# Four buffers instead of two for the output tiles of a fused attention and feed-forward kernel

## The chip, the cores and the metric

The kernel runs on one core of one Trainium2 chip. A core has five engines with instruction streams of their own: PE (TensorE, matrix products; PEld is its loading of weights, which overlaps the products), DVE (VectorE), ACT (ScalarE), POOL (GpSimd) and SP (SyncE, which here issues every DMA, in order). The metric is the device time of one execution in microseconds; where a kernel was run several times the median counts. All matrix products are in float32, most of them split into a high and a low part of type fp32r, so that one product becomes three.

## What is computed

```python
def sm_attn(qq, kk, vv):
    s = scale * np.matmul(qq, kk.transpose(0, 1, 3, 2))
    s = s - np.max(s, axis=-1, keepdims=True)
    a = np.exp(s)
    a = a / (np.sum(a, axis=-1, keepdims=True) + 1e-09)
    return np.matmul(a, vv)
p_packed = sm_attn(p, k, v)            # 32 packed rows per head
out = sm_attn(q, p_packed, p_packed)   # 8 batches, 8 heads, 576 rows, 64 wide
...
h = x @ w_in                           # x: 4608 x 512, w_in: 512 x 2048
g = np.maximum(h, 0.0) + alpha * np.minimum(h, 0.0)
return (g @ w_out).astype(np.float32)  # w_out: 2048 x 512
```

The attention's output, its heads side by side, is the `x` of the feed-forward part.

## The kernel before

The kernel never forms `x`. For each batch, `packed_w` multiplies the packed rows with `w_in` (the result is `pw`, matmuls on lines L435 to L437, copies on L443), and the feed-forward part multiplies that by the second attention's weights (`a_h`, `a_l`).

The feed-forward part works in **sweeps**. A sweep k covers half a batch, 288 tokens, and there are 16. Within one it runs over f = 0 to 15, sixteen blocks of 128 of d_ff. For each f, `first(k, f)` makes a product in a PSUM tile `ps_h` (L480 to L482, six matmuls of 128x288; L468 in the first two sweeps), and takes it through a chain of four steps: ACT forms `neg` (L486), DVE puts the leaky part together in place (L487), ACT rounds it to `gh` (L492), DVE takes the remainder `gl` (L493). There are two `ps_h` buffers and three each of `gh` and `gl`. `second(k, f)` then multiplies `gh` and `gl` by the block f of `w_out` into four accumulators `acc0` to `acc3`, one for each 128 columns of the output (L505, L506 with `gh`, L507 with `gl`, so twelve matmuls for each f). The accumulators are four PSUM banks, each with one buffer, so the next sweep's first product into one of them waits until it has been copied out.

At f = 15 each accumulator is copied into a tile `ot` from the pool `op`: accumulators 0 and 2 by DVE (L524), 1 and 3 by ACT (L522). In the first two sweeps DVE adds a partial sum instead (L518). SP then sends `ot` to memory (L526, 144 KB each). The pool `op` has two buffers; a third copy waits until the first tile's DMA has landed.

For the other matters named below: L456 and L458 split `pw` into `pwh` and `pwl` (on DVE from batch 2 on), once for every two f. L172 and L173 split the attention's inputs (ACT, POOL), L390 to L392 transpose and split the attention's weights (DVE, ACT, POOL). `w` is a block of `w_in`, loaded by L410 into three buffers.

The loops at the end set the program's order of ideas: `first` runs two steps ahead of `second`, and the attention of later batches is spread between them by a table of starting steps. The order on each engine, however, is not that one. A scheduler, with a model of time of its own, deals the instructions to the engines when the program is built; it knows how many buffers a pool has. So a change of a buffer count moves instructions.

Of the kernel before, what the change touches and what calls it, by code (L numbers as in the profile page):

```python
# [28 lines left out]
def pack_attention_ffn_kernel(  # L29
# [42 lines left out]
    pwj = ctx.enter_context(tc.tile_pool(name="pwj", bufs=2))  # L72
    win = ctx.enter_context(tc.tile_pool(name="win", bufs=3))
    gp = ctx.enter_context(tc.tile_pool(name="gp", bufs=2))
    op = ctx.enter_context(tc.tile_pool(name="op", bufs=2))
    dram = ctx.enter_context(tc.tile_pool(name="dram", bufs=1, space=bass.MemoryType.DRAM))
    ps_a = ctx.enter_context(tc.tile_pool(name="ps_a", bufs=1, space=bass.MemoryType.PSUM))
    ps_h = ctx.enter_context(tc.tile_pool(name="ps_h", bufs=2, space=bass.MemoryType.PSUM))
# [555 lines left out]
```

## Time and profile before

| | |
|---|---|
| runs | 836.61, 836.7, 833.1 us; median 836.61 |
| profiled execution | 834.6 us, of which the span from first to last instruction is 832.8 |
| PE busy | 786.3 us, 94% of the span |
| PEld busy | 731.3 us, 88% |
| DVE busy | 610.6 us, 73% |
| ACT busy | 486.6 us, 58% |
| POOL busy | 208.7 us, 25% |
| mean granted TensorE clock | 0.983 of full speed |

Busy time of PE is modelled, and matmuls overlap each other: one of 128x288 is shown with some 300 ns, but the next starts about 130 ns after it. So a delay of PE is best read from the starts of consecutive matmuls, or from the idle time of PEld. A wait is put down to the instruction that released it last. Most waits of DVE and ACT cost nothing, because PE has work in the meantime.

Three stretches follow each other: a prologue of some 170 us in which weights are converted, a middle up to about 628 us in which the feed-forward sweeps share the engines with the attention of later batches, and a late stretch of pure sweeps. Sweeps end in the middle at 243, 293, 341, 387, 433, 485, 534 and 584 us, later at 631, 674, 713, 751, 790, and the last at 827 us.

### The profile page before, as it was taken

To read this page: it belongs to the slowest core of one execution; us is meant where nothing else is said; L and a number is where in the kernel's file an instruction comes from. 1 tells how busy PE (TensorE), PEld (TensorE's weight loads), DVE (VectorE), ACT (ScalarE), POOL (GpSimd) and SP (SyncE) were. 2 spreads that over 40 slices of the span, in tenths; PEclk is the share of its full clock that TensorE was granted. 3 is DMA by queue.
4 is the path that set the end of the run, shared out by engine and by line. 5 is a ranking of instruction groups with operands and counts; after the bars stand their busy time and mean duration, and the time that the engine had idled before them with its cause. 6 is when DMAs were issued, how large, how long until landed. Compare 5 with 4: busy or idle time off the path is not lost.

```text
span 832.8 us, 14967 instructions
## 1 busy us (share of the span) xinstructions
PE 786.3 (94%) x5384; PEld 731.3 (88%) x5384; DVE 610.6 (73%) x1303; ACT 486.6 (58%) x1141; POOL 208.7 (25%) x203
## 2 busy tenths in 40 slices
PE   5489998999999999999999999899999999999997
PEld 3257686898799989998999999899999999999997
DVE  4999798976777657889786487987955566666663
ACT  5778766756666765665667765555655533333332
POOL 2100022536667302353361024533210000000000
PEclk9779999999999999999999999999999999999999
DMA  9877755555623661321227522300262000000000
GB/s 301 280 234 242 240 187 197 195 180 173 209 89 108 207 211 37 91 72 58 61 86 235 199 86 57 89 27 15 80 204 80 26 30 2 29 1 30 2 29 29
DMA packets 55386, 97.97 MB, mean 118 GB/s; under 512 B 5136, under 2 KB 32784, under 8 KB 55312
## 3 DMA queue, kind: packets, MB, share of 16 engines
q1 hardware_dynamic: 55312, 97.02, 36.0%
q8 instruction: 42, 0.69, 0.3%
q14 instruction: 32, 0.26, 0.1%
HBM read 79.18 MB, written 17.83 MB: 116 GB/s over the span
## 4 chain that ended last, share of the span: by engine, by line
PE 71%; DVE 14%; DMA 6%; ACT 5%; issue 2%; SPq 1%; POOL 0%; ACTq 0%; DVEq 0%
PE acc L505 14%; PE acc L506 13%; PE acc L507 13%; PE ps_h L480 6%; PE ps_h L482 6%; PE ps_h L481 6%; PE ps_h L468 2%; PE ps_m L435 2%; PE ps_m L437 2%; PE ps_m L436 2%; DVE ps_h L487 2%; DMA wraw<-in_w_in 1%; PE ps_m L316 1%; DVE pwl L458 1%; DVE mag L127 1%
## 5 line engine op out<-in xcount | busy, mean ns | idle before, releaser
L505 PE MATMUL acc<-gh,wo 128*128 128x288 f32 x1024 | 289.6, 302 | 11.0 <-ACT gh L492 7.9
L506 PE MATMUL acc<-gh,wo 128*128 128x288 f32 x1024 | 283.4, 295 | 0.0
L505 PEld LDWEIGHTS acc<-gh,wo 128*128 128x128 f32 x1024 | 193.0, 189 | 24.1 <-ACT gh L492 15.8
L507 PE MATMUL acc<-gl,wo 128*128 128x288 f32 x1024 | 205.9, 301 | 0.0
L506 PEld LDWEIGHTS acc<-gh,wo 128*128 128x128 f32 x1024 | 193.3, 189 | 1.5
L492 ACT CAST gh<-ps_h 128x288 fp32r<-128x288 f32 x256 | 102.5, 401 | 123.8 <-DVE ps_h L487 113.2
L486 ACT ACTIVATE neg<-ps_h 128x288 f32<-128x288 f32 x256 | 105.6, 413 | 109.0 <-PE ps_h L482 103.0
L493 DVE TENSOR_TENSOR gl<-ps_h,gh 128x288 fp32r<-128x288 f32 x256 | 115.4, 452 | 72.1 <-ACT gh L492 70.4
L487 DVE SCALAR_TENSOR_TENSOR ps_h<-neg,nal,ps_h 128x288 f32<-128x288 f32 x256 | 132.0, 516 | 44.9 <-ACT neg L486 43.3
L507 PEld LDWEIGHTS acc<-gl,wo 128*128 128x128 f32 x1024 | 159.3, 188 | 3.5
L480 PE MATMUL ps_h<-a_h,pwh 128*128 128x288 f32 x448 | 133.5, 298 | 0.3 <-DVE gl L493 0.2
L482 PE MATMUL ps_h<-a_h,pwl 128*128 128x288 f32 x448 | 131.9, 295 | 0.7 <-POOL pwl L458 0.7
L481 PE MATMUL ps_h<-a_l,pwh 128*128 128x288 f32 x448 | 132.0, 295 | 0.0
L173 POOL TENSOR_TENSOR xl<-xraw,xh 128x576 fp32r<-128x576 f32 x48 | 71.0, 1478 | 136.0 <-ACT xh L172 132.8
L480 PEld LDWEIGHTS ps_h<-a_h,pwh 128*128 128x128 f32 x448 | 84.1, 188 | 2.0 <-DVE gl L493 1.0
L482 PEld LDWEIGHTS ps_h<-a_h,pwl 128*128 128x128 f32 x448 | 83.9, 188 | 1.4 <-POOL pwl L458 1.1
L481 PEld LDWEIGHTS ps_h<-a_l,pwh 128*128 128x128 f32 x448 | 84.1, 188 | 0.5
L458 DVE TENSOR_TENSOR pwl<-pw,pwh 128x512 fp32r<-128x512 f32 x96 | 74.5, 776 | 7.1 <-PE ps_h L482 1.2
L456 DVE CAST pwh<-pw 128x512 fp32r<-128x512 f32 x112 | 54.9, 493 | 29.9 <-PE ps_h L481 27.7
L443 ACT COPY pw<-ps_m 64x512 f32<-64x512 f32 x112 | 65.1, 581 | 17.2 <-PE ps_m L437 13.0
L275 POOL TENSOR_TENSOR vs<-vraw,vs 128x640 fp32r<-128x640 f32 x24 | 38.6, 1610 | 42.3 <-ACT vs L274 41.7
L435 PE MATMUL ps_m<-w,pt 128*128 128x512 f32 (+1 forms) x80 | 33.8, 422 | 12.9 <-ACT w L133 10.6
(112 smaller groups left out, 1029.9 us busy)
## 6 DMA issues: line engine op xcount, KB each, us to landing
w<-w_split SPq DMA_DIRECT2D x64, 512.0 KB, 4.2
xraw<-in_kT SPq DMA_DIRECT2D x32, 288.0 KB, 2.9
xraw<-in_qT SPq DMA_DIRECT2D x32, 288.0 KB, 2.8
outT<-ot SPq DMA_DIRECT2D x64, 144.0 KB, 1.8
vraw<-in_v SPq DMA_DIRECT2D x32, 256.0 KB, 2.9
wraw<-in_w_out SPq DMA_DIRECT2D x16, 512.0 KB, 4.1
wraw<-in_w_in SPq DMA_DIRECT2D x16, 512.0 KB, 4.9
w_split<-w SPq DMA_DIRECT2D x16, 512.0 KB, 4.6
```

The source lines that it names most:

```text
L173: nc.gpsimd.tensor_tensor(out=xl, in0=raw, in1=fv(xh), op=ALU.subtract)
L458: eng.tensor_tensor(out=tl, in0=src, in1=fv(th), op=ALU.subtract)
L480: nc.tensor.matmul(ps[:, :HS], th[:, i, fs], a_h[:, i, tok], start=hi, stop=False)
L481: nc.tensor.matmul(ps[:, :HS], th[:, i, fs], a_l[:, i, tok], start=False, stop=False)
L482: nc.tensor.matmul(ps[:, :HS], tl[:, i, fs], a_h[:, i, tok], start=False, stop=lo)
L486: nc.scalar.activation(out=neg, in_=g, func=AF.Relu, scale=-1.0)
L487: nc.vector.scalar_tensor_tensor(out=g, in0=neg, scalar=nal[:, f : f + 1], in1=g, op0=ALU.mult, op1=ALU.add)
L492: nc.scalar.copy(out=gh, in_=g)
L493: nc.vector.tensor_tensor(out=gl, in0=g, in1=fv(gh), op=ALU.subtract)
L505: nc.tensor.matmul(acc[o][:, :HS], wo_t[f][:, 0, os_], gh, start=begin, stop=False)
L506: nc.tensor.matmul(acc[o][:, :HS], wo_t[f][:, 1, os_], gh, start=False, stop=False)
L507: nc.tensor.matmul(acc[o][:, :HS], wo_t[f][:, 0, os_], gl, start=False, stop=end)
```

## The change

The pool `op` gets four buffers in place of two.

```diff
-    op = ctx.enter_context(tc.tile_pool(name="op", bufs=2))
+    op = ctx.enter_context(tc.tile_pool(name="op", bufs=4))
```

No instruction is added or removed; the scheduler's order changes from the second sweep's end onward. In the rows below, a leading + is the order now, - the order before. `acc_9798` to `acc_9801` are accumulators 0 to 3 of the sweep before the last, `acc_10262` to `acc_10265` those of the last; `wo_330` and `wo_390` are the blocks f = 0 and f = 1 of `w_out`.

On PE, where the last sweep begins (at 790 us before; the late sweep ends are alike):

```order
 L506 MATMUL acc_10263<-gh,wo_330 128x288
 L507 MATMUL acc_10263<-gl,wo_330 128x288
+L505 MATMUL acc_10265<-gh,wo_330 128x288
+L506 MATMUL acc_10265<-gh,wo_330 128x288
+L507 MATMUL acc_10265<-gl,wo_330 128x288
+L505 MATMUL acc_10264<-gh,wo_330 128x288
+L506 MATMUL acc_10264<-gh,wo_330 128x288
+L507 MATMUL acc_10264<-gl,wo_330 128x288
 L505 MATMUL acc_10262<-gh,wo_390 128x288
 L506 MATMUL acc_10262<-gh,wo_390 128x288
 L505 MATMUL acc_10263<-gh,wo_390 128x288
 L506 MATMUL acc_10263<-gh,wo_390 128x288
```

The six f = 0 matmuls of accumulators 2 and 3 now stand ahead of the first f = 1 matmul; before, they came after f = 1 and part of f = 2 of accumulators 0 and 1.

On DVE at the same place:

```order
 L524 COPY ot<-acc_9798 128x288
+L524 COPY ot<-acc_9800 128x288
 L458 TENSOR_TENSOR pwl<-pw,pwh 128x512
 L487 SCALAR_TENSOR_TENSOR ps_h<-neg,nal,ps_h 128x288 x2
-L493 TENSOR_TENSOR gl<-ps_h,gh 128x288
-L524 COPY ot<-acc_9800 128x288
-L493 TENSOR_TENSOR gl<-ps_h,gh 128x288
+L493 TENSOR_TENSOR gl<-ps_h,gh 128x288 x2
 L456 CAST pwh<-pw 128x512
 L458 TENSOR_TENSOR pwl<-pw,pwh 128x512
```

The copy of accumulator 2 has moved from behind L458, two L487 and an L493 to right behind the copy of accumulator 0. On ACT the copy of accumulator 3 has moved in the same way, ahead of one L486 and two L492.

On DVE at the sweep end at 534 us, where attention runs beside the sweep (`acc_6477` and `acc_6479` are accumulators 0 and 2; `s_6464` is the transpose that feeds L391 and L392):

```order
-L456 CAST pwh<-pw 128x512
 L390 STREAM_TRANSPOSE s_6464<-t_6575 128x576
+L493 TENSOR_TENSOR gl<-ps_h,gh 128x288
+L456 CAST pwh<-pw 128x512
 L524 COPY ot<-acc_6477 128x288
 L211 TENSOR_TENSOR s_6592<-ps_m,lo 64x288
+L524 COPY ot<-acc_6479 128x288
 L458 TENSOR_TENSOR pwl<-pw,pwh 128x512
 L487 SCALAR_TENSOR_TENSOR ps_h<-neg,nal,ps_h 128x288
 L367 STREAM_TRANSPOSE t_6684<-s_6592 128x576
 L487 SCALAR_TENSOR_TENSOR ps_h<-neg,nal,ps_h 128x288
-L524 COPY ot<-acc_6479 128x288
```

Here too the second copy now comes ahead of L458, and the transpose L390 comes ahead of L456 and of an L493 that stood further up.

## Rows read from the trace of the kernel before

**Rows 1.** Busy time by stretch: us, each engine's busy time (instructions), clock, DMA share, GB/s.

```profile
628.00:826.00 198.00, 197.51 (x1464) 195.15 (x1463) 120.13 (x247) 76.47 (x186) 0.00 (x0) 1.00 0.07 24
190.00:628.00 438.00, 425.88 (x3060) 411.23 (x3060) 327.42 (x708) 277.83 (x652) 170.04 (x153) 1.00 0.36 113
```

**Rows 2.** Tile `ot`: idle time before its instructions, until what (us, times).

```profile
  DMA outT<-ot: 16.5, 17
```

**Rows 3.** Timeline of the tail: start us, us, engine, line, operation [idle before <-releaser].

```profile
826.79 0.46 DVE L524 COPY ot<-acc 128x288 f32<-128x288 f32 x1 [1.36 <-PE acc L507]
...
827.28 3.16 SPq L526 DMA_DIRECT2D outT<-ot  x4
829.14 0.46 DVE L524 COPY ot<-acc 128x288 f32<-128x288 f32 x1 [1.90 <-DMA outT<-ot]
829.60 0.40 ACT L522 COPY ot<-acc 128x288 f32<-128x288 f32 x1 [2.27 <-DMA outT<-ot]
```

**Rows 4.** Timeline of the sweep end at 790 us: DVE's first copy, PE, and `gh`.

```profile
789.82 0.45 DVE L524 COPY ot<-acc 128x288 f32<-128x288 f32 x1
...
790.73 0.29 PE L505 MATMUL acc<-gh,wo 128*128 128x288 f32 x1
...
791.33 0.40 ACT L492 CAST gh<-ps_h 128x288 fp32r<-128x288 f32 x1
791.39 0.30 PE L507 MATMUL acc<-gl,wo 128*128 128x288 f32 x1
...
791.78 0.40 PE L505 MATMUL acc<-gh,wo 128*128 128x288 f32 x1
```

**Rows 5.** Waits of PEld, 628 to 833 us: us in total, times, longest us.

```profile
PEld acc L505 <- ACT gh L492: 1.7, 5, 0.3
```

**Rows 6.** Waits of PEld, 190 to 628 us: six of fourteen rows.

```profile
PEld acc L505 <- ACT gh L492: 9.4, 11, 2.4
PEld ps_m L435 <- ACT gh L492: 1.5, 1, 1.5
...
PEld ps_m L207 <- DVE aT L300: 0.6, 1, 0.6
PEld acc L505 <- ACT ot L522: 0.5, 1, 0.5
PEld acc L505 <- DVE ot L524: 0.4, 1, 0.4
...
PEld acc L505 <- issue: 0.2, 1, 0.2
```

**Rows 7.** Waits of PE, 290 to 300 us.

```profile
PE ps_m L435 <- DMA w<-w_split: 1.3, 1, 1.3
```

**Rows 8.** Waits of PEld, 386 to 440 us: the row on `gh`.

```profile
PEld acc L505 <- ACT gh L492: 0.6, 2, 0.3
```

**Rows 9.** Waits of PEld, 484 to 490 us.

```profile
PEld acc L505 <- ACT gh L492: 0.8, 1, 0.8
```

**Rows 10.** Waits of PEld, 533 to 541 us.

```profile
PEld acc L505 <- ACT gh L492: 2.4, 1, 2.4
```

**Rows 11.** Timeline of the sweep end at 534 us, rows of DVE and POOL.

```profile
532.60 0.46 DVE L493 TENSOR_TENSOR gl<-ps_h,gh 128x288 fp32r<-128x288 f32 x1 [0.30 <-ACT gh L492]
...
533.57 0.43 DVE L456 CAST pwh<-pw 128x512 fp32r<-128x512 f32 x1
...
535.47 1.42 POOL L392 TENSOR_TENSOR a_l<-s,a_h 128x576 fp32r<-128x576 f32 x1 [0.17 <-ACT a_h L391]
...
535.54 1.89 DVE L458 TENSOR_TENSOR pwl<-pw,pwh 128x512 fp32r<-128x512 f32 x1
```

**Rows 12.** Line L458 on DVE: ns min/median/max, first and last start.

```profile
L458 DVE TENSOR_TENSOR pwl<-pw,pwh x96: 672/692/1928, 280.5 to 814.3; 128x512 fp32r<-128x512 f32 x96
```

**Rows 13.** Busy time by stretches of 20 us around 534 us, columns as in rows 1.

```profile
520.00:540.00 20.00, 17.40 (x124) 16.82 (x123) 18.55 (x37) 12.26 (x31) 11.30 (x11) 0.95 0.29 86
540.00:560.00 20.00, 18.95 (x138) 18.71 (x138) 16.10 (x38) 11.47 (x27) 7.33 (x6) 0.96 0.13 39
```

## The prediction, written before the changed kernel was run

> **What bounds the kernel now.** I read the trace in four steps. First the busy time by stretches [rows 1]: after the prologue TensorE (PE) is busy 425.88 of 438 us and then 197.51 of 198 us, and the weight loads beside it (PEld) 411.23 and 195.15. So PE sets the time, and an edit counts only where PE stands still. Second the edited tile: ACT and DVE sat 16.5 us in 17 places until an output DMA had left an `ot` buffer [rows 2]. That is what the change attacks, but it is time of ACT and DVE, not of PE. Third, what PE's weight loads waited for: in the late stretch only the product tile `gh`, 1.7 us in 5 places [rows 5]; in the middle fourteen rows that add up to 19.3 us, the first 9.4 and the last 0.2 [rows 6]. Only two of these name `ot` (0.5 and 0.4). Fourth, the timeline at single sweep ends, to see whether the other waits come from the two buffers after all. They do, in part, and through the order: because the scheduler knew that accumulators 2 and 3 come free late, it placed only the f=0 matmuls of accumulators 0 and 1, six in all, before it asks for `gh` of f=1.
>
> The prologue up to about 170 us has no difference in order and no `ot`; it stays.
>
> **The change part by part.** The number of instructions of each kind is the same. Three things move.
>
> *The tail.* At the last sweep end nothing hides a wait. DVE copies accumulator 0 at 826.79 and accumulator 2 only at 829.14, after 1.90 us of waiting for an output DMA; ACT, free again at 829.60 - 2.27 = 827.33, copies accumulator 3 at 829.60 [rows 3]. With four buffers DVE copies twice in a row, 826.79 + 2 x 0.46 = 827.71, and ACT by 827.33 + 0.40 = 827.73. The last copy ended at 829.60 + 0.40 = 830.00, so the copies gain 2.3. But the four DMA issues then stand in one queue: the four took 3.16 from 827.28 [rows 3], the last thus from 830.0 to 830.44, 0.4 us. Three such ahead of the last put its start at 827.28 + 1.2 = 828.5 in place of 830.0: 1.5. Between 1.5 and 2.3 I take **1.7**, near the issue bound, since that queue comes last.
>
> *Late sweep ends without attention (five: 631 to 790 us).* At the last of them the six f=0 matmuls run from 790.73, the sixth at 791.39, a pitch of 0.66 / 5 = 0.13. The next starts at 791.78, which is 0.39 later: 0.26 lost, because `gh` started only at 791.33 and took 0.40 [rows 4]. All five look alike, 1.7 us of PEld in 5 places [rows 5], about 0.07 more each than PE loses. In the new order twelve matmuls stand there, six more, 6 x 0.13 = 0.79 of cover. Against that, DVE's copy of accumulator 2 now stands ahead of the subtraction L458 and the two L487 that lead to this `gh`. That costs 0.46, so `gh` ends at 791.73 + 0.46 = 792.19, and PE arrives at 790.73 + 12 x 0.13 = 792.3. The wait is gone with 0.1 to spare. What covers the moved copies: DVE's first started at 789.82 [rows 4], so the second ends at 790.74, and PE reaches accumulators 2 and 3 at 790.73 + 0.79 = 791.5. Five times 0.26 is **1.3**; bounds 0 (DVE slower by the 0.1 that is left over, and more) and 1.7.
>
> Idle TensorE weight loads are what the Trainium skill judges this engine by (Perfetto Trace Analysis, "Identifying the Most-Contended Engine": LDWEIGHTS busy time, not matmul busy time). By that page the late stretch has 198 - 195.15 = 2.9 us of headroom at most, and the 16.5 us of waiting on DVE and ACT promise nothing by themselves; the sum would be capped there, not changed.
>
> *Middle sweep ends with attention or packed weights beside them.* The same six extra matmuls stand in, so each wait shrinks by up to 0.79:
> At 293, PE waited 1.3 and PEld 1.5 for a load of `w` [rows 6, 7]; the load lands when it lands, PE gets 0.79 more to do: 0.8 (0 to 1.5).
> At 341, waits of 0.6, 0.4 and 0.2 [rows 6], of which 0.4 is `ot` itself: 0.8 (0.4 to 1.2).
> At 387, 0.5 on `ot` [rows 6] and one of the two 0.3 on `gh` [rows 8]: 0.8.
> At 433, the other 0.3 [rows 8]: 0.3.
> At 485, 0.8 on `gh` [rows 9]: 0.8 (0.3 if the copy moved ahead costs its 0.46).
> At 534, 2.4 on `gh` [rows 10]. Here DVE's L458 took 1.89 instead of the usual 0.692 [rows 11, 12], and it ran over the POOL subtraction L392, 535.47 to 536.89 [rows 11]. If it stays that long, the gain is 0.79 - 0.46 = 0.3. But in the new order two DVE operations (L456 and an L493) go behind the transpose that feeds L392, and a copy comes ahead of L458. L392 starts earlier, L458 later, by about 0.4 + 0.5 + 0.46 = 1.3 together, against an overlap of 1.35. So L458 probably falls back toward 0.692 and I take 0.3 + 1.2 = 1.5. Behind this stall the clock fell to half speed, 0.95 and 0.96 of full speed over two stretches of 20 us [rows 13], that is 1.0 + 0.8 = 1.8 us of lost clock. I leave that in the sum as a loss that stays; its removal is a rival.
> Sum of the six: 0.8 + 0.8 + 0.8 + 0.3 + 0.8 + 1.5 = **5.0**, from 1.5 to 7.0 without the clock.
>
> The Trainium skill (SBUF — State Buffer, "Who interferes with whom") says that a VectorE instruction with two SBUF inputs fully blocks against a GpSimd instruction that reads SBUF, the later one waiting. The 1.89 of L458 beside L392 agrees. By that rule the 534 end gives 1.5 if the two no longer meet and 0.3 if they still do.
>
> *The rest of the middle.* 19.3 less the waits just named (3.8 on `gh`, 1.5, 0.6, 0.5, 0.4, 0.2, together 7.0) leaves 12.3 us of waits inside attention. The order of ACT and DVE is dealt anew there and no row tells which way it falls. I take 0, bounds 3 us either way, a quarter of it.
>
> **Sum:** 1.7 + 1.3 + 5.0 = 8.0. The profiled execution took 834.6 (span 832.8), which makes 826.6. It lies 2.0 below the median of the runs, 836.6, and from the median the sum gives 828.6. I put the forecast between, at 827.5.
>
> **The rivals.**
> *Only the tail.* For it: PE named `ot` for 0.9 us in all [rows 6], and where DVE and ACT wait 16.5 us, PE mostly had work. The `gh` waits might be a property of the DVE chain, which the copy of 0.46 ahead of it lengthens by more than half of the new cover. Then 1.7 plus the 0.9: 834.6 - 2.6 = 832.0, or 834.0 from the median. Against it: the cover of 0.79 exceeds 0.46 wherever the order shows both.
> *The clock fall goes too.* If the stall at 534 sinks far enough, the 1.8 us of half speed go with it and the stall gives 2.4: 826.6 - 0.9 - 1.8 = 823.9, with a lucky deal of the rest 821.
> *Slower: the moved copies push L458 onto POOL's reads.* At seven ends (293 to 584) L458 runs on DVE while POOL is at work. Where L458 now starts 0.46 later, it may meet a POOL subtraction that it missed before: 1.93 at most against 0.692 [rows 12], that is 1.2 + 0.46 - 0.79 = 0.9 lost, and a clock fall of 1.8 behind it, 2.7 per end. It decides once it happens at five of the seven and the middle's 5.0 is lost too: 834.6 + 5 x 2.7 - 3.0 = 845; at three it is 839.7. For it: the 1.89 has happened once. Against: it is one of the 96 in which such a length is the extreme, and the median is 0.692.
> *The change does nothing.* An `ot` buffer might still be held, since all output DMAs pass SP's queue in order. But sweep ends lie many times apart what an output DMA takes to land (1.9 us from 827.28 to 829.14 [rows 3]), and four buffers mean that no copy ever waits for a DMA of its own sweep. Then 834.6 to 836.6.
>
> **How the numbers follow.** The forecast, 824 to 831: 0.56. Only the tail, 831 to 834: 0.22. The clock fall too, 820 to 824: 0.12. Slower: 0.06. Nothing: 0.04. The range runs from 821.5 to 834, which takes in the sums from about 2.5 to 13 and leaves out slower, nothing, and the best of the clock case. A measurement of this kernel can tell about 0.5% from no change, 4.2 us, so faster means below 832.4: 0.56 + 0.12 + 0.04 of the tail case = 0.72. Within 0.5%: 0.22; slower: 0.06.
>
> **What would show it.** In the changed kernel's profile no row of `ot` should wait for an output DMA; the four last copies should end within 1 us of each other; the five late `gh` waits of 0.3 should be gone, and late stretches show PEld busy throughout; at the 534 end L458 should be near 0.7. I am wrong if the 0.3 waits merely move to f=2, if L458 is long in more places, or if the waits inside attention grow by more than 3 us.

## The result and the profile after

The changed kernel takes **824.52 us** (median of 824.1, 824.94, 822.66 and 827.0), beside 834.86 for the kernel before in the same session (831.65 to 836.7): a ratio of **0.9888, 95% interval 0.9862 to 0.9915**. The forecast was 827.5 in a range of 821.5 to 834. The profiled execution took 824.1 us, its span went from 832.8 to 822.0. A second series of the same kernel, described below, gave 824.36.

The stages are cut at the first copy out of an accumulator at a sweep's end, in each profile:

| stage (us) | before | changed | gain |
|---|---|---|---|
| start to the first sweep end (no `ot` yet) | 169.59 | 167.89 | 1.70 |
| first to second sweep end | 12.01 | 12.85 | -0.84 |
| second sweep end to the one at 631 | 449.52 | 443.05 | 6.47 |
| 631 to the last sweep end (five ends) | 195.67 | 193.55 | 2.12 |
| the tail: last sweep end to the span's end | 6.01 | 4.66 | 1.35 |
| span | 832.80 | 822.00 | 10.80 |

The end of the span is printed to a tenth of a microsecond, so tails here are good to 0.05 us. The first line is no part of the change. Its order of instructions is the same in both kernels, and over all profiles of this study, whatever the kernel, that stage took 166.5 to 169.6. So between these two profiles some 1.7 of the 10.8 are chance, and about 9.1 belong to the change, which is 1.1% of the span like the ratio. The order differs from the first sweep's end on, at 170 us, and not only from the second's.

The work is the same, 5384 matmuls with PE busy for 782.6 us (95% of the span); the idle time is less. The two stretches that answer to [rows 1], shifted by the time that was gained (us, busy time of PE, PEld, DVE, ACT and POOL, clock, DMA share, GB/s):

```profile
188.00:618.00 430.00, 421.35 (x3043) 407.42 (x3042) 324.22 (x706) 276.58 (x650) 167.80 (x153) 1.00 0.36 115
618.00:815.00 197.00, 197.00 (x1472) 195.96 (x1471) 121.46 (x250) 77.18 (x187) 0.00 (x0) 1.00 0.07 24
```

PEld stood still for 198 - 195.15 = 2.9 us of the late stretch before and for 197 - 195.96 = 1.0 now. The list of waits of PEld in that stretch, which held one row before [rows 5], is empty. In the middle PEld's idle time went from 26.8 us to 22.6, and its waits, fourteen rows of 19.3 us before [rows 6], are twelve that add up to 15.0. These four lead or bear on what follows (us in all, times, longest):

```profile
PEld acc L505 <- ACT gh L492: 6.1, 10, 1.4
PEld ps_h L480 <- DVE gl L493: 1.9, 4, 0.7
...
PEld acc L505 <- ACT ot L522: 1.0, 2, 0.7
PEld ps_m L294 <- issue: 0.7, 1, 0.7
```

The wait on `gh` fell by a third. Against [rows 2], the tile `ot` has one releaser left ahead of its instructions, the matmul that finishes an accumulator:

```profile
its engine sat idle before it (us, times) until:
  PE acc L507: 4.7, 3
```

And the tail, which answers to [rows 3]:

```profile
817.34 0.82 DVE L524 COPY ot<-acc 128x288 f32<-128x288 f32 x2 [1.36 <-PE acc L507]
817.47 0.70 ACT L522 COPY ot<-acc 128x288 f32<-128x288 f32 x2 [1.98 <-PE acc L507]
...
817.82 1.80 SPq L526 DMA_DIRECT2D outT<-ot  x4
```

All four copies are over 0.83 us after the first began. The four DMA issues, 3.16 before, take 1.80, 0.45 each.

### The profile page after: what moved, and what is told of

The parts are those of the page before. It is cut to its first block, busy times and chain, and to the rows that moved or that the text cites. A ratio compares the mean times of both kernels' runs of the same rounds, so it can differ in the third digit from the quotient of the medians.

```text
span 822.0 us, 14951 instructions
## 1 busy us (share of the span) xinstructions
PE 782.6 (95%) x5384; PEld 729.1 (89%) x5384; DVE 607.2 (74%) x1303; ACT 486.6 (59%) x1141; POOL 206.6 (25%) x203
## 4 chain that ended last, share of the span: by engine, by line
PE 75%; DVE 13%; ACT 5%; DMA 4%; issue 2%; SPq 1%; POOL 0%; ACTq 0%; DVEq 0%
PE acc L505 15%; PE acc L506 14%; PE acc L507 14%; PE ps_h L480 7%; PE ps_h L482 7%; PE ps_h L481 7%; PE ps_m L435 2%; PE ps_m L436 2%; PE ps_m L437 2%; DMA wraw<-in_w_out 2%; PE ps_h L468 1%; PE ps_m L316 1%; DVE ps_h L487 1%; DVE pwl L458 1%; DVE mag L127 1%
## 5 line engine op out<-in xcount | busy, mean ns | idle before, releaser
L507 PE MATMUL acc<-gl,wo 128*128 128x288 f32 x1024 | 201.0, 301 | 0.0
L492 ACT CAST gh<-ps_h 128x288 fp32r<-128x288 f32 x256 | 102.2, 399 | 122.0 <-DVE ps_h L487 120.0
L493 DVE TENSOR_TENSOR gl<-ps_h,gh 128x288 fp32r<-128x288 f32 x256 | 115.5, 452 | 73.9 <-ACT gh L492 72.4
L486 ACT ACTIVATE neg<-ps_h 128x288 f32<-128x288 f32 x256 | 105.4, 412 | 104.8 <-PE ps_h L482 98.8
L487 DVE SCALAR_TENSOR_TENSOR ps_h<-neg,nal,ps_h 128x288 f32<-128x288 f32 x256 | 131.4, 515 | 35.2 <-ACT neg L486 34.2
L480 PE MATMUL ps_h<-a_h,pwh 128*128 128x288 f32 x448 | 133.2, 297 | 1.0 <-DVE gl L493 0.9
L173 POOL TENSOR_TENSOR xl<-xraw,xh 128x576 fp32r<-128x576 f32 x48 | 70.1, 1461 | 134.4 <-ACT xh L172 124.6
L480 PEld LDWEIGHTS ps_h<-a_h,pwh 128*128 128x128 f32 x448 | 84.1, 188 | 2.9 <-DVE gl L493 1.9
L456 DVE CAST pwh<-pw 128x512 fp32r<-128x512 f32 x112 | 55.3, 496 | 35.2 <-PE ps_h L481 33.3
L458 DVE TENSOR_TENSOR pwl<-pw,pwh 128x512 fp32r<-128x512 f32 x96 | 74.7, 778 | 6.6 <-PE ps_h L482 0.8
L210 ACT COPY lo<-ps_m 64x288 f32<-64x288 f32 x96 | 37.8, 395 | 16.9 <-PE ps_m L208 15.4
```

The lines of the kernel that those rows point to most:

```text
L173: nc.gpsimd.tensor_tensor(out=xl, in0=raw, in1=fv(xh), op=ALU.subtract)
L458: eng.tensor_tensor(out=tl, in0=src, in1=fv(th), op=ALU.subtract)
L480: nc.tensor.matmul(ps[:, :HS], th[:, i, fs], a_h[:, i, tok], start=hi, stop=False)
L486: nc.scalar.activation(out=neg, in_=g, func=AF.Relu, scale=-1.0)
L487: nc.vector.scalar_tensor_tensor(out=g, in0=neg, scalar=nal[:, f : f + 1], in1=g, op0=ALU.mult, op1=ALU.add)
L492: nc.scalar.copy(out=gh, in_=g)
```

## What was tested

The theory: the change works through the scheduler's order. With four buffers it may place the f=0 matmuls of accumulators 2 and 3 ahead of f=1, and PE has twelve matmuls in place of six while the chain from `ps_h` to `gh` runs. The gain then comes at every sweep end, 1.35 at the tail, about 0.4 at each of the five late ends, the rest in the middle. The first rival: only the tail gains, the rest is chance or a lucky deal of attention's instructions. The second: it is the buffers alone that help (a copy need not wait), not PE's order.

### One part of the change at a time

Three kernels give the four buffers to some sweep ends alone. At the others accumulators 2 and 3 take tiles from the two old buffers. The tag of `ot` at L516 was changed as follows; `ot_more` is a second pair of buffers. The ends of the first two sweeps, at 170 and 182 us, have two buffers in all three.

```diff
-    to = op.tile([P, HS], F32, name="ot", tag="ot")
+    to = op.tile(..., tag="ot" if k < 15 or o < 2 else "ot_more")            # the tail alone
+    to = op.tile(..., tag="ot" if k < 10 or k > 14 or o < 2 else "ot_more")  # the five late ends alone
+    to = op.tile(..., tag="ot" if k < 2 or k > 9 or o < 2 else "ot_more")    # the eight middle ends alone
```

**The tail alone.**

> Four output buffers in the last sweep alone, two elsewhere; the order on every engine is that of the kernel before. Theory (three separate gains: tail, late ends, middle ends): only the tail moves. The last copy starts within 1 us of the first, in place of 2.8 us behind it, and from the first copy to the end of the span it takes 1.4 to 1.7 us less than the 6.0 of before; the five late waits on gh of 0.3 us and the middle stay. Total 0.998 of before. Rival (the buffers as such give everything, wherever they are): total 0.988.

831.96 us, ratio 0.9977 (0.9963 to 0.9991). The tail takes 4.64 instead of 6.01, the late stretch 195.62 as before. The order of every engine is that of before, so this part is the buffers and nothing else. The issues, from its timeline:

```profile
828.05 1.81 SPq L526 DMA_DIRECT2D outT<-ot  x4
```

**The five late ends alone.**

> Four output buffers at the five sweep ends from 631 to 790 us, two elsewhere. Theory: the five waits of PE's weight loads on gh (1.7 us in all) are gone and the stretch from the copies at 631 to those of the last sweep gets 1.3 to 2.1 us shorter than 195.7; tail and middle as before. Total 0.998. Rival (the late gain is a by-product of what the middle does to the clock or the DMA queue): the late stretch stays 195.7 and the waits stay.

831.94 us, 0.9980 (0.9963 to 0.9997). The late stretch takes 193.52, the changed kernel's 193.55, and PEld has no wait in it; the tail stays at 6.34.

**The eight middle ends alone.**

> Four output buffers at the eight sweep ends from 243 to 584 us, two elsewhere. Theory: most of the gain is here, 5 to 7 us between the copies at 182 and those at 631 (449.5 before), late waits and tail as before; total 0.993. Rival (the middle is only a new deal of the order inside attention, of either sign): within 2 us of before, 0.998 to 1.002.

827.93 us, 0.9930 (0.9911 to 0.9949). The middle takes 444.48 instead of 449.52; late stretch and tail stay at 195.63 and 6.13, with the waits of before in both. From its list of waits in the late stretch (623.5 to 820 us):

```profile
PEld acc L505 <- ACT gh L492: 1.7, 5, 0.3
```

and from the timeline of its tail, where DVE's second copy still waits for a DMA (ACT's does too):

```profile
821.51 0.46 DVE L524 COPY ot<-acc 128x288 f32<-128x288 f32 x1 [1.89 <-DMA outT<-ot]
```

The three shares are 0.0023, 0.0020 and 0.0070, together 0.0113; the change itself is 0.0112. Each is known to 0.0014 to 0.0019 either way. Within that the parts add up, and six tenths lie in the middle. The rival by which only the tail gains has fallen.

### The changed kernel again

> The changed kernel once more, as the measure for the three runs beside it. Theory: 0.988 of before; late stretch 193.5 us, no wait on gh there, and no fall of the clock at the sweep end near 528 us. If that fall is a matter of chance (rival to its being gone with the stall), it may be there this time.

824.36 us, 0.9899 (0.9884 to 0.9914). Its late stretch is 193.55 and its tail 4.68, as in the first profile. No wait on `gh` came back in the late stretch, and the clock did not fall at the end near 528 us. Its middle is 444.56 instead of 443.05, which is chance. Over the five profiles that have the order of before up to 631 us that stage took 448.3 to 451.0, over the five with the changed kernel's order 443.1 to 444.6. The means, 449.6 and 443.9, lie 5.7 apart, so some of the 6.47 in the table is luck.

### Three buffers

```diff
-    op = ctx.enter_context(tc.tile_pool(name="op", bufs=2))
+    op = ctx.enter_context(tc.tile_pool(name="op", bufs=3))
```

> Three output buffers everywhere. Theory: the third accumulator is freed in time and the fourth is not, so PE has three more matmuls ahead of f=1 (0.39 us of cover), which is above the late loss of 0.26; the late waits go, the tail's last copy still waits some 1.5 us, and the total lies two thirds of the way, about 0.991 to 0.994. Rival (only all four buffers change the order): total 0.998 to 1.0.

830.81 us, 0.9971 (0.9955 to 0.9986). That is a quarter of the gain, less than was expected. The tail's last copy starts 2.79 after the first, as before (2.81): the fourth copy waits as the third and fourth did. The late stretch takes 196.77, which is 1.1 *longer* than with two buffers. Its waits there, and a late end from its timeline:

```profile
PEld acc L505 <- ACT ot L522: 1.6, 1, 1.6
PEld acc L505 <- ACT gh L492: 1.5, 5, 0.3
```

```profile
787.50 0.40 ACT L492 CAST gh<-ps_h 128x288 fp32r<-128x288 f32 x1
787.60 0.29 PE L507 MATMUL acc<-gl,wo 128*128 128x288 f32 x1
...
787.95 0.40 PE L505 MATMUL acc<-gh,wo 128*128 128x288 f32 x1
```

PE has nine matmuls there now, 0.39 more cover than before. But DVE makes both its copies ahead of the chain, and `gh` starts 1.9 after the first of them, at 785.6, instead of 791.33 - 789.82 = 1.5 [rows 4]. `gh` still starts just ahead of PE's last covered matmul, and PE still stands for 0.35 - 0.13 = 0.22. The third buffer's cover is used up by the copy that it allows to move forward; only the fourth brings more than it costs there. One wait of 1.6 on ACT's copy, fourth in line for three buffers, comes on top.

### Buffers without PE's order

In two kernels with four buffers PE was held back at the five late ends, by an edge that sets an order and adds no wait of its own. `behind(a, b)` puts `a` after `b`. In the program's text, too, the f=0 products of accumulators 2 and 3 were moved behind f=1 of accumulators 0 and 1 there.

```diff
+    # half: accumulator 2's f=0 matmuls go behind f=1 of accumulators 0 and 1
+    k > 10 and f == 0 and o == 2 and behind(m5, held[k, 1, 1][1])
+    # both: accumulators 2 and 3
+    k > 10 and f == 0 and o > 1 and behind(m5, held[k, 1, 1][1])
```

**Half held.** This was meant to hold both, and held the three matmuls of accumulator 2 only; those of accumulator 3 stayed ahead of `gh`.

> The changed kernel with four buffers, but at the five late sweep ends PE is held to the order of before: the f=0 matmuls of accumulators 2 and 3 behind those of f=1 of accumulators 0 and 1. DVE, ACT and SP keep the order of the change. Theory (the six extra matmuls on PE are the cover, and the copy moved ahead on DVE costs 0.45): waits on gh come back at the five ends, at 0.26 + 0.4 = 0.67 us each, some 3.3 us, and the late stretch is 3 us longer than in the changed kernel. Rival (free buffers shorten the wait themselves, the order on PE is indifferent): the late stretch stays 193.5.

827.29 us, 0.9935 (0.9918 to 0.9952); late stretch 195.11 instead of 193.55. A late end from its timeline:

```profile
784.22 0.29 PE L505 MATMUL acc<-gh,wo 128*128 128x288 f32 x1
...
785.28 0.29 PE L507 MATMUL acc<-gl,wo 128*128 128x288 f32 x1
...
785.63 0.40 PE L505 MATMUL acc<-gh,wo 128*128 128x288 f32 x1
```

With nine matmuls the wait is 785.63 - 785.28 - 0.13 = 0.22, where twelve left none. The size expected for all six matmuls was missed because only three were taken back.

**Both held.** So the edge was put on both accumulators.

> As e7_order_held, but with the f=0 matmuls of both accumulators 2 and 3 held behind f=1 of accumulators 0 and 1 at the five late ends (e7_order_held held those of accumulator 2 alone, so three of the six extra matmuls stayed). The copies stay ahead on DVE and ACT; later in those sweeps one pair of L487 and L493 changes places. Theory (each matmul less of cover is 0.13 of wait): 0.39 more at each end than in e7_order_held, so the late stretch is 2 us longer than its 195.1, about 197, and 3.5 longer than the 193.55 of the changed kernel. Rival (the wait depends on the copies, not on the matmuls): 195.1 again.

828.19 us, 0.9938 (0.9912 to 0.9963); late stretch **197.15**, as expected, 3.6 more than in the changed kernel. Its only wait there, and a late end:

```profile
PEld acc L505 <- ACT gh L492: 3.5, 5, 0.7
```

```profile
786.07 0.30 PE L507 MATMUL acc<-gl,wo 128*128 128x288 f32 x1
786.83 0.40 PE L505 MATMUL acc<-gh,wo 128*128 128x288 f32 x1 [0.46 <-ACT gh L492]
```

193.55, 195.11, 197.15 for 0, 3 and 6 matmuls held at five ends: 0.31 and 0.41 per end and step, near 3 x 0.13 = 0.39 each. With the buffers and without the order the late stretch is 1.5 *worse* than before (195.67), because DVE's second copy still stands ahead of the chain. PE's gap is 786.83 - 786.07 - 0.13 = 0.63 in place of 0.26, so the copy costs 0.37, less than its length of 0.45: two copies in a row take 0.82 (817.34 above).

### PE's order without the buffers

Two kernels with two buffers put f=0 of all four accumulators ahead of f=1 at the late ends.

```diff
+    # first: f=1 of accumulator 0 goes behind f=0 of accumulator 3
+    k > 10 and f == 1 and o == 0 and behind(m5, held[k, 0, 3][2])
+    # whole: f=1 of accumulators 0 and 1 does, and the product for f=3 (L480) too
+    k > 10 and f == 1 and o < 2 and behind(m5, held[k, 0, 3][2])
+    k > 10 and f == 3 and i == 0 and behind(m, held[k, 0, 3][2])
```

> The kernel before with two buffers, but at the five late ends PE is made to do the f=0 matmuls of all four accumulators ahead of f=1, as in the change. Theory (the order needs the buffers): PE waits for the copies of accumulators 2 and 3, which wait for a DMA: accumulator 2 is free at 792.69 where PE arrives at 791.52, so 1.2 us lost per end in place of 0.26, and the late stretch is 4 to 5 us longer than the 195.7 of before. Rival (the order alone is the gain, the buffers only let the scheduler find it): 1.3 to 2 us shorter than before.

836.08 us, 1.0038 (1.0023 to 1.0053); late stretch 197.63 instead of 195.67. It was not the test that it was meant to be: the scheduler moved f=1 of accumulator 1 and the next product ahead in place of what was held, and most of PE's order was as before. So the edge was completed.

> As e8_order_two, with the hold made complete: with two buffers, PE does the f=0 matmuls of all four accumulators ahead of f=1 of accumulators 0 and 1 and ahead of the next product of first. DVE, ACT and SP are those of the kernel before, word for word. (In e8_order_two the f=1 matmuls of accumulator 1 and the next product still went ahead.) Theory (the new order needs the buffers): PE stands at accumulator 2 until its copy ends, 1.2 us per end in place of 0.26, the late stretch 200 or more against 195.7. Rival (the order alone is the gain): 193.5 to 194.5.

839.38 us, **1.0073** (1.0052 to 1.0095); late stretch 202.45, 6.8 more than before, with the instructions of DVE, ACT and SP in the order of before. Its waits there, and a late end:

```profile
PEld acc L505 <- DVE ot L524: 6.7, 5, 1.5
PEld acc L505 <- ACT ot L522: 0.5, 1, 0.5
```

```profile
797.20 0.45 DVE L524 COPY ot<-acc 128x288 f32<-128x288 f32 x1
797.70 0.19 PEld L505 LDWEIGHTS acc<-gh,wo 128*128 128x128 f32 x1 [1.29 <-DVE ot L524]
```

Four of the five ends lost 0.8 to 1.0 each, the one at 674 us 3.1. There the wait on ACT's copy came on top, and behind it the granted clock was at half speed for 3.4 us. The sweep from that end, and the next (us, busy time of PE, PEld, DVE, ACT and POOL, clock, DMA share, GB/s):

```profile
674.07:715.71 41.64, 40.15 (x291) 39.67 (x290) 24.56 (x52) 13.59 (x35) 0.00 (x0) 0.96 0.05 16
715.71:755.24 39.53, 38.49 (x291) 38.25 (x290) 24.37 (x51) 13.58 (x35) 0.00 (x0) 1.00 0.05 16
```

Of the 2.1 between them the second wait and a longer first one explain some 0.7; about 1.4 is left for the clock (an estimate; 3.4 us at half speed are 1.7). So the order itself cost some 5 of the 6.8.

The wait now bears the name of `ot`. It is the same shortage that stood under the name of `gh` before: in the order of before PE waits 0.26 for `gh`, and in this one 1.3 for the copy that waits for an `ot` buffer, so with two buffers the scheduler's order was the better one. Neither the buffers nor the order gives the late gain alone; together they do.

### One middle end alone

The sweep end at 534 us before, the one with the longest stall, was given the four buffers by itself (tag `"ot" if k != 8 or o < 2 else "ot_more"`).

> Four output buffers only at the sweep end at 534 us (k=8), two elsewhere. There DVE's second copy stands ahead of L458 as in the change, but the transpose L390 stays behind L456, as before. Theory (L458 is long because it runs over POOL's L392, and in the change it is the earlier L390 that separates them): the copy alone shifts L458 by 0.45 of the 1.35 us of overlap, so it stays over 1.3 us long, PE's wait on gh shrinks from 2.2 to about 1.4 us by the six more matmuls, and the interval to the next end goes from 49.9 to 49.1. Rival (the free buffer alone does it): L458 near 0.7, PE's wait under 1 us, the interval 48.4 as in the changed kernel.

833.18 us, 0.9996 (0.9976 to 1.0017). From its timeline at that end:

```profile
535.95 1.43 POOL L392 TENSOR_TENSOR a_l<-s,a_h 128x576 fp32r<-128x576 f32 x1 [0.23 <-ACT a_h L391]
...
536.33 1.59 DVE L458 TENSOR_TENSOR pwl<-pw,pwh 128x512 fp32r<-128x512 f32 x1
...
538.84 0.40 PE L505 MATMUL acc<-gh,wo 128*128 128x288 f32 x1 [1.63 <-ACT gh L492]
```

L458 is still long over L392, and PE stands 1.63 (2.20 before). From this end to the next it took 49.4 us instead of 49.9, where 49.1 was expected; the stretch behind that took 47.5 instead of 47.0. So half a microsecond was gained and handed on: at the next end, 584 us, PE now stands 0.49 for `gh`, where it did not stand before. The transpose L390 comes behind L456 here, as before; in the changed kernel, where earlier sweeps have changed too, it comes ahead, and L458 is short. So this end's own buffers alone do not give its gain. That it is L390's place that does was not tried by itself.

### Two queues for the last outputs

Whether the issue queue still binds the tail was tried on the changed kernel: in the last sweep ACT issues the DMAs of accumulators 1 and 3.

```diff
-    nc.sync.dma_start(out=outT[...], in_=to)
+    (nc.scalar if k == 15 and o % 2 else nc.sync).dma_start(out=outT[...], in_=to)
```

> The changed kernel with the output DMAs of accumulators 1 and 3 of the last sweep issued by ACT instead of SP. Theory (after the change the four issues in one queue are what is left of the tail, 1.80 us): two issues side by side, so the span ends 0.7 us sooner after the first copy than the 4.66 us of the changed kernel. Rival (the DMA's landing, not its issue, sets the end): no difference. In the total it cannot be told apart.

824.61 us, 0.9900 (0.9885 to 0.9915): no faster than the changed kernel. From its timeline, and then the time from issue to landing of the last four output DMAs, in the changed kernel and in this one:

```profile
818.50 0.81 SPq L526 DMA_DIRECT2D outT<-ot  x2
818.58 0.86 ACTq L526 DMA_DIRECT2D outT<-ot  x2
```

```profile
DMA to landing us min/median/max: 1.7/1.8/1.8
DMA to landing us min/median/max: 1.7/2.1/2.4
```

The last issue is over 818.58 + 0.86 - 818.50 = 0.94 after the first began instead of 1.80, but the tail is only 0.28 shorter (4.38), where 0.7 was expected: the last transfer took 2.4 to land instead of 1.8, and that ate most of what the issues gained. So the landing bounds this tail too, as the rival says. No version tried here beats the changed kernel.

## Why the prediction was right, and where it was not

The forecast came out 3 us high, with the right mechanism. Part of the 3 lies in where it started: the first three runs of the kernel before gave 836.6, and 58 later ones, in three series, have medians of 832.7 to 833.2. In the later series the change was worth 832.69 - 824.36 = 8.3 us, close to the sum of 8.0, though not term by term. Counted from the profiled execution the sum gave 826.6, and the changed kernel's profiled execution took 824.1. The 2.8 by which the 10.8 exceeds the sum of 8.0 are 1.7 of chance in the prologue, 0.8 of the late ends, and 1.47 in the middle, less 0.35 of the tail and 0.84 of the second sweep end. By its terms:

**What bounds the kernel.** Right: PE, and only where it stands. The 16.5 us that ACT and DVE waited for buffers are gone and brought 1.35 in the tail; all else came from PE's idle time, of which rows under another name than `ot` held most. The Trainium skill's measure (Perfetto Trace Analysis, "Identifying the Most-Contended Engine") capped the late stretch at 2.9 us of idle weight loads; 2.85 - 1.04 = 1.8 of them were won, so the traces agree.

**The tail: 1.7 forecast, 1.35 measured.** The issue queue did come last, as said. The term for it was too small: 0.4 per issue was read from the single last issue of before, while four in a row took 1.80, 0.45 each, and 3.16 - 1.80 = 1.36. The 1.7 was set above the issue bound of 1.5 by choice; no row asked for that.

**The late ends: 1.3 forecast, 2.1 measured.** All five waits went, and no other came. The term 0.26 per end was too small, 0.42 in fact. It measured only the gap in front of the stalled matmul and took PE to run on at 0.13 behind it. The trace of before shows otherwise; from the same sweep end as [rows 4], with the matmul that stalled until 791.78:

```profile
791.78 0.19 PEld L505 LDWEIGHTS acc<-gh,wo 128*128 128x128 f32 x1 [0.33 <-ACT gh L492]
791.87 0.45 DVE L493 TENSOR_TENSOR gl<-ps_h,gh 128x288 fp32r<-128x288 f32 x1
792.02 0.29 PE L506 MATMUL acc<-gh,wo 128*128 128x288 f32 x1
...
792.37 0.19 PEld L480 LDWEIGHTS ps_h<-a_h,pwh 128*128 128x128 f32 x1
792.41 0.36 PE L480 MATMUL ps_h<-a_h,pwh 128*128 128x288 f32 x1
...
792.61 0.29 PE L481 MATMUL ps_h<-a_l,pwh 128*128 128x288 f32 x1
```

From the stalled matmul to the next it is 792.02 - 791.78 = 0.24, which is 0.11 over the pitch: its weight load waited too and started only with it, where it otherwise starts 0.13 ahead. And 792.61 - 792.41 = 0.20, another 0.07, is a second small wait: L480 needs the `ps_h` buffer that L493 reads last, L493 ends at 791.87 + 0.45 = 792.32, and the weight load starts at 792.37. 0.26 + 0.11 + 0.07 = 0.44 per end. The prediction had noted that PEld waits 0.07 longer at each end than PE loses, and went by PE. In the changed kernel DVE makes both copies first here too, but the first `gh` (two in a row, 0.41 each) ends at 783.07. The matmul that needs it starts at 783.31, its weight load 0.13 sooner, at 783.18: 0.1 to spare, as forecast, though by two slips that cancel: the copy was charged 0.46 and costs 0.37, and the weight load was not asked for. No gap is left:

```profile
780.77 0.82 DVE L524 COPY ot<-acc 128x288 f32<-128x288 f32 x2
...
782.66 0.82 ACT L492 CAST gh<-ps_h 128x288 fp32r<-128x288 f32 x2 [0.29 <-DVE ps_h L487]
...
783.18 0.19 PEld L505 LDWEIGHTS acc<-gh,wo 128*128 128x128 f32 x1
783.31 0.29 PE L505 MATMUL acc<-gh,wo 128*128 128x288 f32 x1
```

The cover of 0.79 against the copy's 0.46 was the right comparison; holding three and six matmuls back and giving three buffers each showed it from another side.

**The middle: 5.0 forecast for six ends, 5.2 measured.** What the stretch from each of these ends to the next gained:

| end (us, before) | 293 | 341 | 387 | 433 | 485 | 534 |
|---|---|---|---|---|---|---|
| forecast | 0.8 | 0.8 | 0.8 | 0.3 | 0.8 | 1.5 |
| measured | 1.1 | 0.9 | 0.8 | 0.9 | 0.0 | 1.5 |

That the sum comes so close is luck in part: 0.8 too much at 485 stands against 0.3 too little at 293 and 0.6 at 433. The 1.1 and the 0.9 at 433 are also the loose ones. Over all profiles with the order of before at these ends the two stretches took 47.0 to 48.2 and 51.8 to 53.1, and 46.8 to 47.1 and 50.8 to 51.4 with the new order.

At all eight middle ends the timeline of PE shows six f=0 matmuls ahead of the first f=1 before, and twelve in the changed kernel. At 293, 341 and 387 PE's stops of 1.3, 0.4 and 0.3 us are gone. But no run held PE's order back in the middle. That the buffers give the gain there is shown by the eight ends alone; that they give it through the cover is read from these rows and was not tested as at the late ends, so a lucky deal of attention's instructions is not ruled out for a part of it.

**At 485 the step failed.** It put the gain on `gh` and did not ask what PE meets next. The wait on `gh` is gone [rows 9], but 0.3 on a copy to `ot` and another stop took its place. From the changed kernel's timeline of PE, that end being at 480 now:

```profile
483.43 0.52 PE L294 MATMUL ps_m<-ident,s_t 128*128 128x128 f32 x3 [0.45 <-DVE s_t L268]
```

A transpose of attention waits for DVE's scaling of the softmax, 0.45 (in PEld's list above it is the 0.7 on L294). Together 0.75, as much as was won. That end was not tried by itself.

**The 534 end.** Its 1.5 came, and L458 fell to 0.68 as forecast. But DVE still met POOL there, now with the cast L456 in front. From the changed kernel's timeline, that end being at 528 now:

```profile
527.12 1.44 POOL L173 TENSOR_TENSOR xl<-xraw,xh 128x576 fp32r<-128x576 f32 x1 [0.79 <-ACT xh L172]
...
527.41 1.44 DVE L456 CAST pwh<-pw 128x512 fp32r<-128x512 f32 x1
...
528.50 1.61 POOL L392 TENSOR_TENSOR a_l<-s,a_h 128x576 fp32r<-128x576 f32 x1
...
530.10 0.68 DVE L458 TENSOR_TENSOR pwl<-pw,pwh 128x512 fp32r<-128x512 f32 x1
```

L456 takes 1.44 over POOL's L173, 0.43 before [rows 11]. PE now has several short stops up to the next end in place of a long one (waits of PE, 526 to 578 us):

```profile
PE acc L505 <- ACT gh L492: 1.4, 2, 1.2
PE acc L505 <- DVE ot L524: 0.5, 1, 0.5
PE ps_h L480 <- DVE gl L493: 0.5, 1, 0.5
```

Together 2.4. With the order of before and no fall of the clock it stood 2.20, 1.46 and 0.39, together 4.05 (the first kernel with two buffers and PE's late order).

**The rest of the middle: 0 forecast.** From the first sweep end to the second the new order takes 0.84 more, in every profile that has it, and the sweep behind that 0.9 less, so these two cancel. What is left of the 6.47, 0.4, is no more than chance: the stretch from 243 to 293 took 50.0 us in the first profile of the changed kernel and 51.4 in the second, beside 50.4 before.

**The lost clock.** The prediction left the fall to half speed behind the stall at 534 [rows 13] as 1.8 us that stay, and made their removal a rival. Both readings are wrong. The fall is absent from all kernels with the new order there, and with it or without it that stretch takes the same time. Busy time from that sweep end to the next, columns as in rows 1: the kernel before, and then the first kernel with two buffers and PE's late order, whose order up to there is that of before and whose clock did not fall:

```profile
534.19:584.11 49.92, 46.67 (x343) 46.08 (x342) 39.21 (x89) 28.45 (x71) 19.62 (x16) 0.97 0.13 37
```

```profile
531.70:581.69 49.99, 45.85 (x343) 44.80 (x342) 40.67 (x89) 28.46 (x72) 19.39 (x16) 1.00 0.13 37
```

49.92 at a clock of 0.97, 49.99 at 1.00. Over all five profiles with that order it is 49.8 to 50.1 with the fall (three) and 49.98 and 49.99 without (two). Where the clock did not fall, PE reaches the next thing that it waits for sooner and waits longer (before, 1.05 at 547.7; without the fall 1.46 and 0.39). DVE sets the pace there: without the fall it is busy 12.48 of the 13.14 us behind the stall, PE 11.20. That 824.5 lies near the rival's 823.9 has other reasons: the late term, and 1.7 us of chance in the prologue.

**The slower rival.** L458 did meet POOL in new places: from 274 us on, before has eleven instances of L458 and five of L456 that took over 0.9 us, 22.0 us together; the changed kernel has nine and five, 21.5 us. The longest now takes 2.05, 1.93 before [rows 12]. Its mechanism is real, but it strikes as often as it spares. **The change does nothing** fell with the first look at `ot`.

## What to carry to other kernels

When a scheduler that knows the pools sets the order, a short pool may stand in the profile under another tile's name: it is found by asking which work would cover the wait, and why it is not placed there. What such an edit is worth is the added cover (matmuls times their pitch) less what the edit moves ahead of the chain that is waited for; a third buffer can cost what it gives where a fourth pays. A stop of PE is worth more than the gap in front of the stalled matmul, since its weight load was held up too and is no longer hidden. A fall of the clock may be worth nothing where PE would have waited for another engine soon after, and cost most of the time that it takes from PE where PE alone sets the pace.

## What the runs showed of the hardware

- Behind a stall the next matmul starts 0.24 us after the stalled one, with a pitch of 0.13 otherwise. It is so at all five late ends of the kernel before (gap 0.26), with three matmuls held back (0.22), with six (0.63) and in the order without the buffers (1.2 to 1.4). So each of these stalls cost 0.11 more than its gap, short or long.
- The granted clock fell to half speed (1.2 instead of 2.4 GHz) for 3.4 us behind the stall of 2.20 at 534 us, in the kernel before, with the tail alone and with the late ends alone; it did not in the two kernels with PE's order and two buffers, whose order there is the same. There the fall cost nothing, 49.92 against 49.99. In a late sweep of the second of those two kernels (behind the end at 674 us) a fall of the same length cost about 1.4 us, by the estimate above.
- A cast is stretched over a POOL subtraction as a subtraction with two inputs from SBUF is: L456 from 0.43 to 1.44, L458 from 0.69 to 1.59 and 1.89. The Trainium skill (SBUF — State Buffer, "Who interferes with whom") names both, the cast where it runs in a mode that takes both ports. For L458 the traces agree; in which mode L456 ran no run here shows.
- Four output DMAs of 144 KB issued in a row by one queue take 0.45 us each. Over two queues they are issued in half the time, but take up to 2.4 instead of 1.8 to land, which leaves 0.28 of the 0.86.
